# One bank more held back before a score tile is issued, in the last 24 visits of a fused attention and token-mixing kernel

## The chip, the cores and the metric

The kernel runs on one core of one Trainium2 chip. The metric is the device time of one launch in microseconds. Before the change three runs took 1613.73 to 1614.21 us, with a median of 1614.09 us.

## The reference, cut to what matters

```python
def _A_ref(x, wq, wk, wv, wo):            # 32 heads of 20, one key and one value for all of them
    q = (x @ wq).reshape(B, S, H, Dh).transpose(0, 2, 1, 3)
    k = x @ wk
    v = x @ wv
    scores = jnp.einsum("bhqd,bkd->bhqk", q, k) * (Dh ** -0.5)
    p = _softmax(scores, axis=-1)
    o = jnp.einsum("bhqk,bkd->bhqd", p, v)
    return o.transpose(0, 2, 1, 3).reshape(B, S, H * Dh) @ wo
def _B_ref(x, w1, b1, w2, b2):            # an MLP over the tokens
    h = _layernorm(x, axis=-1)
    u = _gelu(jnp.einsum("bsd,sf->bdf", h, w1) + b1)
    return (jnp.einsum("bdf,fs->bds", u, w2) + b2).transpose(0, 2, 1)
g = _sigmoid((x * gate_w).sum(-1, keepdims=True))
out = g * _A_ref(x, ...) + (1 - g) * _B_ref(x, ...)
```

S is 2048 tokens, D 640 channels, F 1728; everything is float32.

## The kernel before, in words

**Visits.** Attention is worked off in 32 units (4 blocks of 512 queries times 8 groups of 4 heads), and each unit in 16 visits, one for every 128 keys: 512 visits. A visit has four score tiles (line 643, a 62-row matmul of 128 keys by 512 queries), each followed by an exponential on ScalarE (line 652, `p<-...`), and then the product with v (line 754, written `PV` below) on the whole array. The softmax's row maxima are found ahead of time: line 494 makes score tiles with the queries as rows, and VectorE takes their maxima (line 500). The maxima of a whole unit go through lines 515 (VectorE), 517 to 519 (GpSimd), 526 (VectorE), 527 (a store to DRAM, on SyncE's queue) and 533 (the fetch back, on the same queue) into two rows of the unit's query tile, from which the score matmuls read them.

**Halves.** Score tiles and the long products of the MLP and of the output projection use only 64 of the array's 128 rows. Two of them run at the same time, one in the upper half (rows 0 to 63) and one in the lower (64 to 127). TensorE takes its instructions in one program order; an instruction that waits holds up everything behind it, of both halves.

**Banks.** PSUM has 8 banks of 128x512 float32, with the tile names `ms` (three), `s` (three), `g` and `o`. In the last stretch one of them (`o`) collects the products with v over all visits; the other seven go round between score tiles, tiles for row maxima, and the accumulators of the output projection. A bank comes free when the exponential, the maximum or the closing sum (line 934, VectorE) has read it.

**The last 24 visits.** The first 488 visits are arranged by the function `main`, the last 24 by a loop of their own from line 1230 on, in eight blocks of 2, 3, 3, 3, 3, 3, 3 and 4 visits. What stands beside the scores there is the output projection of the last tokens (`tail_job`, line 926): chains of half-array products (64x128 by 64x320), written `L926` below. Each chain opens an accumulator with its first product, and needs a free bank for it; the chain's end calls line 934. A block first issues its score tiles (`lanes[b]`, for half `b`; in the first two blocks the last tiles for row maxima too) and its share of the products (`fs[b]`, pairs of the instruction and of whether it opens an accumulator), mixed by the rule that is changed, and then the PV of its visits, back to back. The scores run one visit ahead of the PV. How many scores and products a block has in each half is settled before the mixing.

**The planner's clock.** `at[b]` is the planner's own time of half `b`; a score advances it by `X_US` 0.232 and a product by `F_US` 0.147. `pool` holds the free banks, each with the time at which the planner expects it to be free; `bank_take` takes the earliest, `bank_give` returns it with the time at which its reader should be done. `banks_at(t)` counts the banks that are free by `t`. The loop of one block:

```python
while any(lanes) or any(fs):
    b = 0 if at[0] <= at[1] and (lanes[0] or fs[0]) or not (lanes[1] or fs[1]) else 1
    soon = sum(any(first for _, first in f[:3]) for f in fs)
    score = lanes[b] and (not fs[b] or banks_at(at[b]) > soon)
    if score or fs[b][0][1]:
        at[b] = max(at[b], min(e for e, _ in pool))
    clock["now"] = at[b]
    if score:
        lanes[b].pop(0)()
        at[b] += X_US
    else:
        fs[b].pop(0)[0]()
        at[b] += F_US
```

So `soon` is the number of halves (0, 1 or 2) that open an accumulator among their next three products.

Of the kernel before, what the change touches and what calls it, by code (L numbers as in the profile page):

```python
# [44 lines left out]
def mix_kernel(ctx: ExitStack, tc: tile.TileContext, A_x, A_wq, A_wk, A_wv, A_wo,  # L45
# [436 lines left out]
    def ms_next(b):  # L482
        k = given[b]
        if k >= 32 * NU:
            return None
        given[b] += 1
        n, r = divmod(k, 32)
        (kq, pr), qt = divmod(r // 4, 2), r % 4

        def step():  # L490
            if n not in mtiles:
                mtiles[n] = mpool.tile([P, 16, 4], F32, name="mp")
            ms = lead_bank() if lead_banks else bank_take()
            nc.tensor.matmul(ms, qmax[n][64 * b:64 * b + 60, pr, qt * P:(qt + 1) * P],  # L494
                             kst[64 * b:64 * b + 60, kq * NB:(kq + 1) * NB], start=True, stop=True)
            if not lead_banks:
                bank_give(ms, "max")
            c = (2 * b + pr) * 4 + qt
            behind, last["ins"] = last["ins"], None
            r = nc.vector.tensor_reduce(mtiles[n][:, c, kq:kq + 1], ms, axis=AX.X, op=ALU.max)  # L500
            if behind is not None:
                tc.add_manual_dep(r.ins, behind.ins.name, SYNC, reason="row tiles that share a bank")
                last["sig"] = r
            issued[b] += 1
            if min(issued) == 32 * n + 1:
                new_qmax(n + 1)

        return step

    def ms_done():  # L510
        n = len(row_max)
        if n < NU and min(issued) >= 32 * (n + 1):
            mm = mmpool.tile([P, 16], F32, name="mm")
            busy("dve", 0.14)
            nc.vector.tensor_reduce(mm, mtiles.pop(n), axis=AX.X, op=ALU.max)
            mn = mmpool.tile([P, 2, 16], F32R, name="mn")
            nc.gpsimd.tensor_scalar(mm, mm, -1.0, None, op0=ALU.mult)
            nc.gpsimd.tensor_copy(mn[:, 0, :], mm)
            nc.gpsimd.tensor_sub(mn[:, 1, :], mm, f32(mn[:, 0, :]))
            row_max[n] = mn  # L520

    def store_max(n):
        mn = row_max[n]
        mt = mpool.tile([P, 32], F32, name="mt")
        busy("dve", 0.19)
        nc.vector.transpose(mt, f32(mn).rearrange("p j c -> p (j c)"))
        nc.sync.dma_start(out=m_scr[n].rearrange("m (i e) -> i m e", i=4), in_=mt)

    def fetch_max(n):
        src = m_scr[n].rearrange("(j b r) e -> b j (r e)", j=2, b=2)  # L530
        for b in range(2):
            rows = f32(qtiles[n][64 * b + 60:64 * b + 62])
            nc.sync.dma_start(out=rows.rearrange("j p q -> j (p q)"), in_=src[b])
# [90 lines left out]
    def s_next(b):  # L624
        j = sc[b]
        if j >= 2 * len(units):
            return None
        sc[b] += 1

        def step():  # L630
            qk(j // 2, j % 2, b)

        step.score = True
        return step
# [31 lines left out]
    at, skip, final = 0, 3, NS * PRO - 6  # L666
# [65 lines left out]
    def banks_at(t):  # L732
        return sum(e <= t for e, _ in pool)
# [151 lines left out]
    def tail_load(i, late=False):  # L885
        st, r0, r1 = jobs[i]
        cols = slice(st * P, (st + 1) * P)
        oT, yt = room(i)
        c1 = r1 // P
        for j in range(2):  # L890
            if r0:
                low = slice(r0 + j * MID // 2, r0 + (j + 1) * MID // 2)
                nc.sync.dma_start(out=f32(oT[:MID, j, 0]), in_=o_scr[j, r0:r1, cols])
                nc.sync.dma_start(out=f32(oT[MID:MID * 3 // 2, j, 0]), in_=o_scr[0, low, cols])
            elif not late:
                nc.sync.dma_start(out=f32(oT[:, j, :c1]), in_=o_scr[j, :c1 * P, cols].rearrange("(c p) s -> p c s", p=P))
            else:
                nc.sync.dma_start(out=f32(oT[:r1 - c1 * P, j, c1]), in_=o_scr[j, c1 * P:r1, cols])
        if r0 == 0 and not late:
            nc.sync.dma_start(out=yt, in_=y_scr[cols, :])  # L900
            if r1 < D:
                nc.gpsimd.memset(f32(oT[r1 - c1 * P:, :, c1, :]), 0.0)
        if late or r0 or r1 == D:
            loaded.append(i)

    def load_mid():
        for j, t in enumerate(wo_mid):
            for w, r0, r1, at in ((wo_hi, 0, MID, 0), (wo_lo, j * MID // 2, (j + 1) * MID // 2, MID)):
                while r0 < r1:
                    c, r = divmod(CUT + r0, P)  # L910
                    n = min(r1 - r0, P - r)
                    nc.sync.dma_start(out=f32(t[at:at + n]), in_=f32(w[r:r + n, c, :]))
                    r0, at = r0 + n, at + n
# [33 lines left out]
    def tail_take(h, n):  # L947
        out = []
        while len(out) < n and tail[h] and tail[h][0][0] in loaded:
            out.append(tail[h].pop(0)[1:])  # L950
        return out
# [54 lines left out]
    def full_last():  # L1006
        ws = [ev.tile([P, NB], F32, name="part", bufs=2) for _ in range(2)]
        for d, w in enumerate(ws):
            nc.gpsimd.memset(w[:, :HD2], 0.0)
            for hh in range(4):  # L1010
                r = (H - 4 + hh) * DH
                nc.sync.dma_start(out=w[32 * hh:32 * hh + DH, :HD2], in_=A_wo[r:r + DH, d * HD2:(d + 1) * HD2])
        return ws
# [79 lines left out]
    def settle(wide=False):  # L1093
        for _ in range(2 if spare[0] else 1):
            if later and (wide or spare[0] or not later[0][0]):
                f = later.pop(0)[1]
                if f:
                    f()
        pop_chain()
# [20 lines left out]
    lanes = [0.0, 0.0]  # L1120
# [109 lines left out]
    for j, n in enumerate(BLOCKS):  # L1230
        ends = [min(2 * len(units), 2 * (v + n) + 2) for _ in range(2)]
        lanes = [[], []]
        own = [(2 * len(units) - c + 32 * NU - m) * X_US for c, m in zip(sc, given)]
        while any(sc[b] < ends[b] for b in range(2)):
            b = int(sc[1] < sc[0])
            lanes[b].append(s_next(b))
        for b in range(2):
            more = -(-(32 * NU - given[b]) // max(1, LAST_M - j))
            for i in range(more):
                lanes[b].insert((i + 1) * len(lanes[b]) // (more + j), ms_next(b))  # L1240
        left = len(units) - v
        fs = [tail_take(b, len(tail[b]) if n == left else
                        max(0, round(((own[b] + len(tail[b]) * F_US) * n / left - len(lanes[b]) * X_US) / F_US)))
              for b in range(2)]
        at = [begin, begin]
        while any(lanes) or any(fs):
            b = 0 if at[0] <= at[1] and (lanes[0] or fs[0]) or not (lanes[1] or fs[1]) else 1
            soon = sum(any(first for _, first in f[:3]) for f in fs)
            score = lanes[b] and (not fs[b] or banks_at(at[b]) > soon)
            if score or fs[b][0][1]:  # L1250
                at[b] = max(at[b], min(e for e, _ in pool))
            clock["now"] = at[b]
# [6 lines that stand above are left out]
        begin = max(at) + 0.38 + n * 0.927  # L1259
        ms_done()  # L1260
        for _ in range(n):
            settle()
            pv_group([v], True)
            v += 1
        if NU - 1 in set(row_max) - sent:
            store_max(NU - 1)
            sent.add(NU - 1)
            fetch_max(NU - 1)
            back_in.add(NU - 1)
        if v - n < 492 <= v:  # L1270
            load_mid()
        if v - n < 498 <= v:
            w_full = full_last()
        if v >= 502 and len(loaded) < len(jobs):
            for i in range(len(loaded), len(jobs)):
                tail_load(i)
# [94 lines left out]
```

## Time and profile before

| what | before |
|---|---|
| median of 3 runs | 1614.09 us |
| time of the profiled execution | 1613.95 us |
| its span | 1612.2 us |
| TensorE busy | 1605.3 us (100%) |
| VectorE, ScalarE, GpSimd busy | 1355.9, 1308.0, 868.4 us |
| granted TensorE clock | 1.000 |
| stretch of the last 24 visits | 1531 to 1601 us of the span |

How to read it: the time is that of the whole launch, the span runs from the first to the last instruction in the trace, and 1.75 us lie around it. "Busy" of TensorE counts every moment at which at least one matmul is under way in either half, and the ends of matmuls are modelled; so a stretch in which one half stands still, or in which both do for a tenth of a microsecond, shows as busy.

### The profile page before, as it was taken

The page shows a single profiled execution, that of the slowest core. Times are in us where ns is not written, and L with a number is a line of the kernel's source. Part 1 is how long each engine was busy: PE and PEld are TensorE (multiplying, and loading weights), DVE is VectorE, ACT ScalarE, POOL GpSimd, SP SyncE. Part 2 cuts the span into 40 slices and gives each one's busy share as a digit, 9 for nine tenths or more (in the row PEclk, how much of TensorE's full clock was granted, in tenths as well). Part 3 has the DMA queues.
Part 4 walks back from the last instruction along what each step waited for, and adds up shares of the span by engine and source line. Part 5 has one row for each costly group of instructions (what it writes and reads, how often), then busy time and mean ns, then how long its engine had stood idle before and what let it go on. Part 6 is the DMA issues. An engine that isn't in the chain of part 4 may idle for free.

```text
span 1612.2 us, 39502 instructions
## 1 busy us (share of the span) xinstructions
PE 1605.3 (100%) x14865; PEld 1124.5 (70%) x14865; DVE 1355.9 (84%) x2344; ACT 1308.0 (81%) x2565; POOL 868.4 (54%) x977
## 2 busy tenths in 40 slices
PE   9999999999999999999999999999999999999998
PEld 7889777677767776666666666666666666666676
DVE  6689999999999999888888888888888888766643
ACT  4445888888888888888888888888888888999974
POOL 6568766778767777644544434454544433344420
PEclk9999999999999999999999999999999999999999
DMA  7655323223233323222222122222222212346421
GB/s 216 212 164 143 78 73 80 76 75 87 77 86 84 80 66 83 64 73 81 73 71 68 51 66 66 72 70 81 73 73 73 59 48 67 96 119 188 151 85 50
DMA packets 183750, 145.07 MB, mean 90 GB/s; under 512 B 38291, under 2 KB 145424, under 8 KB 183560
## 3 DMA queue, kind: packets, MB, share of 16 engines
q1 hardware_dynamic: 183272, 142.23, 31.6%
q8 instruction: 117, 1.92, 0.5%
q14 instruction: 73, 0.60, 0.1%
q10 hardware_dynamic: 288, 0.33, 0.1%
HBM read 108.75 MB, written 32.15 MB: 87 GB/s over the span
## 4 chain that ended last, share of the span: by engine, by line
PE 98%; DVE 1%; POOL 0%; ACT 0%; issue 0%; DVEq 0%; POOLq 0%
PE s L754 16%; PE g L832 11%; PE s L643 10%; PE ms L754 10%; PE g L1035 9%; PE ms L643 8%; PE ms L494 7%; PE s L494 6%; PE pp L303 4%; PE o L754 4%; PE o L643 3%; PE o L494 2%; PE s L686 2%; PE g L971 2%; PE ms L926 1%; DVE mp L500 1%
## 5 line engine op out<-in xcount | busy, mean ns | idle before, releaser
L500 DVE TENSOR_REDUCE mp<-ms 128x1 f32<-128x512 f32 x966 | 632.2, 680 | 59.3 <-PE ms L494 50.9
L652 ACT ACTIVATE p<-s 128x512 f32<-128x512 f32 x941 | 545.7, 618 | 44.5 <-PE ms L754 12.8
L500 DVE TENSOR_REDUCE mp<-s 128x1 f32<-128x512 f32 x756 | 499.8, 680 | 74.1 <-PE s L494 61.2
L652 ACT ACTIVATE p<-ms 128x512 f32<-128x512 f32 x817 | 482.2, 615 | 37.0 <-PE s L754 13.6
L767 POOL TENSOR_TENSOR acc<-acc,part 128x512 f32<-128x512 f32 x213 | 275.1, 1291 | 313.4 <-ACT part L766 300.7
L494 PE MATMUL ms<-kst,qmx 60*128 60x512 f32 x966 | 378.6, 413 | 0.1
L643 PE MATMUL s<-qst,kst 62*128 62x512 f32 x946 | 363.4, 408 | 0.2 <-DVE mp L500 0.2
L643 PE MATMUL ms<-qst,kst 62*128 62x512 f32 x822 | 322.2, 408 | 0.7 <-DMA qst<-m_scr 0.7
L1035 PE MATMUL g<-slot,wh 64*128 64x320 f32 x1344 | 306.1, 313 | 0.0
L494 PE MATMUL s<-kst,qmx 60*128 60x512 f32 x756 | 302.3, 413 | 0.0
L754 PE MATMUL s<-p,v_sb 128*32 128x512 f32 x2240 | 269.4, 598 | 0.0
L1035 PEld LDWEIGHTS g<-slot,wh 64*128 64x128 f32 x1344 | 216.7, 184 | 69.6 <-issue 52.0
L500 DVE TENSOR_REDUCE mp<-o 128x1 f32<-128x512 f32 x303 | 206.2, 681 | 42.9 <-PE o L494 41.4
L134 POOL TENSOR_TENSOR wl<-wr,wh 128x512 fp32r<-128x512 f32 (+1 forms) x176 | 218.0, 1239 | 30.6 <-ACT wh L131 15.4
L643 PEld LDWEIGHTS s<-qst,kst 62*128 62x128 f32 x946 | 174.1, 185 | 60.8 <-ACT p L652 27.0
L1035 PE MATMUL g<-slot,wl 64*128 64x320 f32 x672 | 205.4, 306 | 0.0
L832 PE MATMUL g<-u,wh 64*128 64x320 f32 x864 | 196.5, 309 | 0.0
L832 PE MATMUL g<-slot,wh 64*128 64x320 f32 x864 | 196.3, 309 | 0.0
L643 PEld LDWEIGHTS ms<-qst,kst 62*128 62x128 f32 x822 | 151.5, 186 | 46.8 <-ACT p L652 29.3
L494 PEld LDWEIGHTS ms<-kst,qmx 60*128 60x128 f32 x966 | 175.3, 185 | 4.2 <-DVE mp L500 0.4
L652 ACT ACTIVATE p<-o 128x512 f32<-128x512 f32 x264 | 162.7, 616 | 11.3 <-PE ms L754 7.1
L754 PE MATMUL ms<-p,v_sb 128*32 128x512 f32 x1344 | 161.6, 598 | 0.0
(250 smaller groups left out, 3078.6 us busy)
## 6 DMA issues: line engine op xcount, KB each, us to landing
wr<-in_B_w_dram SPq DMA_DIRECT2D x136, 256.0 KB
qmx<-q_scr SPq DMA_DIRECT2D x192, 80.0 KB
qst<-q_scr SPq DMA_DIRECT2D x192, 80.0 KB
ot<-l_scr SPq DMA_DIRECT2D x120, 64.0 KB
y_scr<-yo SPq DMA_DIRECT2D x16, 320.0 KB
slot<-o_scr SPq DMA_DIRECT2D x16, 320.0 KB
o_scr<-ot SPq DMA_DIRECT2D x124, 40.0 KB
o_scr<-acc SPq DMA_DIRECT2D x124, 40.0 KB
```

Source lines behind the costliest of these rows:

```text
L134: nc.gpsimd.tensor_sub(wl[:, :nv], wr[:, :nv], f32(wh[:, :nv]))
L303: nc.tensor.matmul(pp, w, t, start=first and n == 0, stop=not more and n == len(steps) - 1)
L494: nc.tensor.matmul(ms, qmax[n][64 * b:64 * b + 60, pr, qt * P:(qt + 1) * P], kst[64 * b:64 * b + 60, kq * NB:(kq + 1) * NB], start=True, s ...
L500: r = nc.vector.tensor_reduce(mtiles[n][:, c, kq:kq + 1], ms, axis=AX.X, op=ALU.max)
L643: nc.tensor.matmul(s, kst[64 * b:64 * b + 62, kb * P:(kb + 1) * P], q[64 * b:64 * b + 62, pr, :], start=True, stop=True)
L652: e = nc.scalar.activation(p, s, AF.Exp, scale=SCALE)
L686: nc.tensor.matmul(pu[r][:, :HD2], w[rows, c, :], h[rows, st, :], start=(st == 0 and k == 0), stop=(st == NS - 1 and k == 2))
L754: nc.tensor.matmul(o[32 * hh:32 * hh + 32, :], v_sb[:, kb + i, :], ptiles.pop((u, hh)), start=opened and i == 0, stop=(i == len(us) - 1) a ...
L767: nc.gpsimd.tensor_add(sums[0], sums[0], part)
L832: other_tile(half, nc.tensor.matmul(hold["p"][:, :HD2], w[r, i, :], u[d][r, fc, :], start=(hold["n"] == 1), stop=(hold["n"] == 6 * FC - 3)))
L971: other_tile(half, nc.tensor.matmul(hold["p"][:, :HD2], o[r, c, :], w[r, c, d * HD2:(d + 1) * HD2], start=(hold["n"] == 1), stop=(hold["n" ...
L1035: other_tile(half, nc.tensor.matmul(hold["p"][:, :HD2], w[r, st % HS, :], h[d][r, st, :], start=(hold["n"] == 1), stop=(hold["n"] == 6 * NS)))
```

## The change

A score tile (or a tile for row maxima, which goes through the same list) is issued only while more than `soon + 1` banks are free by the planner's clock, where more than `soon` were enough. A half that has no products left issues its scores as before.

```diff
             soon = sum(any(first for _, first in f[:3]) for f in fs)
-            score = lanes[b] and (not fs[b] or banks_at(at[b]) > soon)
+            score = lanes[b] and (not fs[b] or banks_at(at[b]) > soon + 1)
             if score or fs[b][0][1]:
                 at[b] = max(at[b], min(e for e, _ in pool))
```

The numbers of scores, maxima and products in each block and half stay what they were, as do the orders of GpSimd's and SyncE's instructions. On TensorE the mixture inside each of the eight blocks changes, and with it the banks that the tiles get. Two places follow.

On TensorE, the start of the fourth block, just behind the last product with v of the third. A row is one instruction (x2: two in a row): its line, its output tile, its inputs. `L643` is a score, `L926` a product; the half isn't shown. Before:

```order
L643 MATMUL ms<-qst,kst 128x512
L643 MATMUL s<-qst,kst 128x512
L643 MATMUL ms<-qst,kst 128x512
L643 MATMUL s<-qst,kst 128x512
L643 MATMUL ms<-qst,kst 128x512
L926 MATMUL g<-slot_84,u_1163 128x320 x2
L926 MATMUL s<-slot_84,u_1163 128x320
L926 MATMUL g<-slot_84,u_1163 128x320
L926 MATMUL s<-slot_84,u_1163 128x320
L926 MATMUL g<-slot_84,u_1163 128x320
L926 MATMUL s<-slot_84,u_1163 128x320
L926 MATMUL g<-slot_84,u_1163 128x320
```

The same place after:

```order
L643 MATMUL ms<-qst,kst 128x512
L643 MATMUL g<-qst,kst 128x512
L643 MATMUL s<-qst,kst 128x512 x2
L926 MATMUL ms<-slot_84,u_1163 128x320
L926 MATMUL s<-slot_84,u_1163 128x320
L926 MATMUL ms<-slot_84,u_1163 128x320
L926 MATMUL s<-slot_84,u_1163 128x320
L926 MATMUL ms<-slot_84,u_1163 128x320
L926 MATMUL s<-slot_84,u_1163 128x320
L926 MATMUL ms<-slot_84,u_1163 128x320
L926 MATMUL s<-slot_84,u_1163 128x320
```

Before, five scores stand ahead of the first product, and with the two accumulators (`g` and `s`) that makes seven banks; after, four scores stand there, and the fifth comes behind five products of its half. The blocks 3 and 5 to 8 start in the same two ways.

On VectorE, around the end of the second block: `L500` are the last row maxima of the last unit, `L934` the closing sums of accumulators (a pair for each half of an output tile), `L515` and `L526` the steps that follow the last maximum. Before:

```order
L934 SCALAR_TENSOR_TENSOR yo<-g,g_col,yo 128x320
L500 TENSOR_REDUCE mp<-ms 128x1 x3
L934 SCALAR_TENSOR_TENSOR yo<-s,g_col,u_1163 128x320
L934 SCALAR_TENSOR_TENSOR yo<-s,g_col,yo 128x320
L500 TENSOR_REDUCE mp<-s 128x1
L515 TENSOR_REDUCE mm<-mp 128x16
L526 STREAM_TRANSPOSE mt<-mn 128x32
```

After:

```order
L934 SCALAR_TENSOR_TENSOR yo<-g,g_col,yo 128x320
L500 TENSOR_REDUCE mp<-s 128x1
L500 TENSOR_REDUCE mp<-g 128x1
L500 TENSOR_REDUCE mp<-ms 128x1
L934 SCALAR_TENSOR_TENSOR yo<-ms,g_col,u_1163 128x320
L934 SCALAR_TENSOR_TENSOR yo<-ms,g_col,yo 128x320
L500 TENSOR_REDUCE mp<-s 128x1
L500 TENSOR_REDUCE mp<-g 128x1
L515 TENSOR_REDUCE mm<-mp 128x16
L526 STREAM_TRANSPOSE mt<-mn 128x32
```

One more maximum stands behind the second pair of sums than before, so two maxima instead of one follow it ahead of `L515`.

## The prediction

> **What bounds the kernel now.** I read the page's chain first, then the busy time in the eight blocks of the last 24 visits, then one block instruction by instruction. The chain that ended last, by engine:
>
> ```profile
> PE 98%; DVE 1%; POOL 0%; ACT 0%; issue 0%; DVEq 0%; POOLq 0%
> ```
>
> TensorE's instruction stream is the kernel; a tenth of a microsecond taken out of it comes off the time. The change reaches only the stretches of the last 24 visits in which scores and products are mixed. They are, as the chain in order of time has them, the stretches between the end of one run of PV and the start of the next (columns: length; busy time and count of TensorE, its weight loads, VectorE, ScalarE, GpSimd; TensorE's granted clock; DMA share; GB/s):
>
> ```profile
> 1531.41:1535.45 4.04, 4.04 (x47) 3.69 (x50) 3.15 (x5) 3.99 (x9) 3.77 (x4) 1.00 0.19 76
> 1537.31:1543.53 6.22, 6.22 (x69) 5.70 (x73) 4.98 (x9) 5.76 (x12) 0.02 (x1) 1.00 0.30 78
> 1546.24:1552.24 6.00, 6.00 (x72) 5.52 (x75) 2.05 (x4) 5.47 (x12) 0.00 (x0) 1.00 0.30 70
> 1554.95:1560.93 5.98, 5.98 (x72) 5.52 (x75) 2.40 (x5) 5.51 (x12) 0.00 (x0) 1.00 0.02 4
> 1563.65:1569.60 5.95, 5.95 (x71) 5.54 (x75) 1.46 (x4) 5.49 (x12) 2.51 (x4) 1.00 0.30 69
> 1572.31:1578.34 6.03, 6.03 (x72) 5.61 (x76) 1.73 (x4) 5.57 (x12) 0.00 (x0) 1.00 0.27 75
> 1581.05:1586.95 5.90, 5.90 (x71) 5.43 (x74) 2.20 (x4) 5.43 (x12) 0.00 (x0) 1.00 0.01 3
> 1589.66:1597.83 8.17, 8.17 (x97) 7.41 (x100) 3.55 (x7) 5.99 (x12) 0.00 (x0) 1.00 0.01 2
> ```
>
> The eight lengths add up to 48.3 us. All of them read as 100% busy, which hides the question: whether both halves of the array work all the time. The timeline of TensorE in the fourth block tells (start, duration, line, output<-inputs):
>
> ```profile
> 1554.88 0.50 PE L643 MATMUL ms<-qst,kst 62*128 62x512 f32 x1
> 1554.88 0.50 PE L643 MATMUL s<-qst,kst 62*128 62x512 f32 x1
> 1555.22 0.40 PE L643 MATMUL ms<-qst,kst 62*128 62x512 f32 x1
> 1555.22 0.40 PE L643 MATMUL s<-qst,kst 62*128 62x512 f32 x1
> 1555.45 0.39 PE L643 MATMUL ms<-qst,kst 62*128 62x512 f32 x1
> 1555.46 0.45 PE L926 MATMUL g<-slot,u 64*128 64x320 f32 x2
> 1555.68 0.31 PE L926 MATMUL s<-slot,u 64*128 64x320 f32 x1
> ...
> 1555.98 0.31 PE L926 MATMUL s<-slot,u 64*128 64x320 f32 x1
> ...
> 1556.13 0.43 PE L643 MATMUL ms<-qst,kst 62*128 62x512 f32 x1
> ...
> 1557.54 0.50 PE L643 MATMUL s<-qst,kst 62*128 62x512 f32 x1
> ...
> 1557.88 0.41 PE L643 MATMUL g<-qst,kst 62*128 62x512 f32 x1
> ...
> 1558.44 0.50 PE L643 MATMUL s<-qst,kst 62*128 62x512 f32 x1
> ...
> 1559.45 0.30 PE L926 MATMUL s<-slot,u 64*128 64x320 f32 x1
> ...
> 1560.04 0.31 PE L926 MATMUL s<-slot,u 64*128 64x320 f32 x1
> ...
> 1560.48 0.45 PE L926 MATMUL ms<-slot,u 64*128 64x320 f32 x2
> 1560.86 0.64 PE L754 MATMUL o<-p,v_sb 128*32 128x512 f32 x4
> ```
>
> Four numbers come out of it. A product takes its half 0.1475 us (1559.45 to 1560.04 are four steps). A score takes 0.233 (1555.22 to 1555.45 to 1555.68 in the first half, 0.46 for two). The block's first score takes 0.34, 0.107 more, and lasts 0.50 instead of 0.39 or 0.40. From the last product (the second of 1560.48, so 1560.63) to the first PV it is 0.23, 0.08 more than a product's step.
>
> With these the least length of a block is known, since the program's order tells how many scores and products each half gets: in the fourth block 6 and 27 in one, 6 and 28 in the other. The fuller half needs 6 x 0.233 + 28 x 0.1475 = 5.53, and with 0.107 and 0.08 it is 5.72. It took 5.98; 0.26 are waits. The same for each block (scores and products of the fuller half: 7 and 14; 10 and 22; 6 and 28 in blocks 3 to 6; 6 and 27; 6 and 40) gives least lengths of 3.88, 5.76, four times 5.72, 5.57 and 7.49, together 45.6. **The eight blocks hold 2.7 us that are neither work nor unavoidable**: 0.16, 0.46, 0.28, 0.26, 0.23, 0.31, 0.33 and 0.68. That is all that another mixture can gain.
>
> **What makes up the 2.7 us.** The readers of the banks in the fourth block, ScalarE's exponentials and VectorE's first sums:
>
> ```profile
> 1555.42 0.60 ACT L652 ACTIVATE p<-ms 128x512 f32<-128x512 f32 x1 [2.66 <-PE s L643]
> 1555.91 0.59 ACT L652 ACTIVATE p<-s 128x512 f32<-128x512 f32 x1
> 1556.39 0.60 ACT L652 ACTIVATE p<-ms 128x512 f32<-128x512 f32 x1
> 1556.86 0.62 ACT L652 ACTIVATE qmx<-s 128x512 f32<-128x512 f32 x1
> ...
> 1557.18 0.55 DVE L934 SCALAR_TENSOR_TENSOR yo<-g,g_col,u 128x320 f32<-128x320 f32 x1 [1.47 <-PE g L926]
> 1557.83 0.55 DVE L934 SCALAR_TENSOR_TENSOR yo<-s,g_col,yo 128x320 f32<-128x320 f32 x1
> ```
>
> The exponentials begin 0.54 after the first score and follow every 0.48; a bank is back 0.60 later. Five scores and two accumulators take all seven banks by 1555.68. The sixth score, due at 1556.13 (0.15 behind the product of 1555.98), needs the first exponential's bank, which ends at 1556.02, and lasts 0.43 instead of 0.39. The score of 1557.54 needs the fourth exponential's (1556.86 + 0.62 = 1557.48); the one of 1558.44 needs the second sum's (1557.83 + 0.55 = 1558.38). Each starts 0.06 behind its bank's last reader, lasts 0.50 like a block's first score, and holds up the next score of its half: 1557.54 to 1557.88 are 0.34 where 0.233 would do. So even a wait of a few hundredths costs about 0.1 us, and the instructions of the other half behind it come late as well.
>
> **The change part by part.** It removes and adds no instruction. It moves the fifth score of a block behind five products or more (the fourth block's order shows it), and so leaves a bank free at each later issue.
>
> Walked through for the fourth block, in time from its first score: scores at 0 and 0.34 in both halves, then products from 0.575. The exponentials still begin at 0.54 and free banks at 1.20, 1.68, 2.17 and 2.66 (0.06 behind the ends above). Two accumulators and four scores leave one bank free, and the fifth score, at 0.575 + 5 x 0.1475 = 1.31, finds that one and the bank of 1.20. The next two accumulators open at about 2.0 and 2.1 and find the other one and that of 1.68. The next scores come at about 2.7 and 2.9 and find the banks of 2.17 and 2.66; the ones after that, from 3.2 on, the sums' banks, from about 2.9. Nothing waits: the block takes its least 5.72, and 0.26 are gained.
>
> The same walk, with the same durations (0.43 from a score's start to an idle reader's, which is the 0.54 without the first score's 0.107; 0.65 from sum to sum; 0.69 a maximum, from a row further down), through the other new blocks leaves ten waiting instructions: four in block 2, one each in 3 and 5, two each in 6 and 8. They cost 0.22, 0.11, 0.07, 0.27 and 0.15, together 0.8. Some blocks now end with a lone score in one half, where before they ended with products in both; I put 0.2 for that over all blocks. **The sum: 2.7 gone, 0.8 + 0.2 back, 1.7 us gained.** This is an estimate, and its ends are 2.7 (nothing waits any more) and 0 (as many waits as before, at other places); below 0 one mechanism is known, which is the slower rival. I take the walk's value, since the fourth block's waits come out of the same steps as the trace has them.
>
> What is moved later is covered. A score that comes later makes its exponential later, but the last four scores of a block belong to the next block's PV, and ScalarE's twelve exponentials at 0.48 take 5.8 of the 8.7 us between the starts of the fourth and the fifth block. In the last block, whose scores are all needed, the last scores now stand ahead of some 16 products of their half, 2.3 us, and the fourth visit's PV is last in its run. SyncE's and GpSimd's orders don't move. VectorE's sums move with the products; their readers wait for nothing near.
>
> One rule of the Trainium skill bears on the mixture. Two products of one half that follow each other directly are the pair of 1555.46: 0.45 for both, so 0.31 for one and 0.15 to the next, no more than across the halves. The Trainium skill (TensorE: Matmul & The Clock Gate, Part 3, The mechanism) says that a weight load overlaps with running matmuls only when its row group differs, so each such pair would show a load; the trace disagrees. By that rule, with 62 direct neighbours of one half in the old order and 53 in the new, 9 x 0.107 = 1.0 us more would be gained; I leave it out of the sum.
>
> **The rivals.** (1) *The waits only move* (no gain, 1613.6 to 1614.4 us). The planner's clock runs from its own estimate of each block's start, and where it is off by a tenth the spare bank is counted wrongly. For it: in the old order the clock let the sixth score go at the very moment its bank came back. Against: one whole bank more is about 0.48 us of slack, one exponential's step, and the waits are hundredths.
>
> (2) *All waits go* (2.7 us, 1611.4). For it: the fourth block's walk. Against: the second block, where five tiles for maxima go round beside the twelve scores, and the last.
>
> (3) *The last unit's maxima come late* (slower). The last maximum goes through VectorE, GpSimd, a store and a fetch; until that has landed, TensorE's whole queue stands at the first score of the last unit, in the third block. The chain, on VectorE, SyncE's queue and TensorE:
>
> ```profile
> 1542.47 0.69 DVE L500 TENSOR_REDUCE mp<-s 128x1 f32<-128x512 f32 x1
> 1543.20 0.22 DVE L515 TENSOR_REDUCE mm<-mp 128x16 f32<-128x64 f32 x1
> 1544.37 0.21 DVE L526 STREAM_TRANSPOSE mt<-mn 128x32 f32<-128x32 f32 x1 [0.95 <-POOL mn L519]
> 1544.61 0.56 SPq L527 DMA_DIRECT2D m_scr<-mt  x1
> 1546.58 0.53 SPq L533 DMA_DIRECT2D qst<-m_scr  x2
> 1548.65 0.42 PE L643 MATMUL s<-qst,kst 62*128 62x512 f32 x1
> 1548.91 0.47 PE L643 MATMUL g<-qst,kst 62*128 62x512 f32 x1
> ```
>
> The score of 1548.91 is the first reader, 5.75 us behind the end of the last maximum (1543.16), and it came 0.26 behind the score before it in its half, so it waited at most 0.03. In the new order the third block starts about 0.4 earlier and the reader stands 3.4 us into it, at 1549.2, so there are at least 0.3 us of room; the last maximum, now with another one ahead of it behind the second pair of sums, is due between the same time and 0.6 later. At 0.6 this costs 0.3. Slower than before it gets from a delay of 2.0 on; two more pairs of sums ahead of the maxima (four times 0.65) would be 2.6, and the kernel 0.6 slower, 1614.7. To be 0.2% slower takes 5.3 us of delay, about a whole second chain.
>
> **How the numbers follow.** The profiled execution took 1613.95 us, 0.14 less than the median of 1614.09. It would take 1613.95 - 1.7 = 1612.25, and the median 1612.4 us. Chances: the forecast, 0.9 to 2.4 us gained, 0.64; rival 1 0.16; rival 2 0.08; rival 3 0.08; 0.04 for something that the trace doesn't show. The range takes in rivals 1 and 2 and the near part of 3: 1611.3 to 1614.5. A difference of 0.2% is 3.2 us, about what a measurement of this kernel can tell from no change. The forecast and rivals 1 and 2 lie within it, since the blocks hold only 2.7; beyond it on the faster side I leave 0.06, for something outside the blocks, and on the slower side 0.07, mostly rival 3 at its worst.
>
> **What would show it.** Right: the eight stretches add up to about 46.6 us instead of 48.3, the fourth is near 5.72, and scores of 0.43 to 0.50 behind a block's first pair become rare. Right in mechanism but wrong in size: they are rare, yet the blocks keep their lengths. Wrong: a gap before a score in the third block that ends with the fetch of the maxima, PV that waits for an exponential, or a difference outside 1531 to 1601 us.

## The result, and the profile after

The changed kernel takes 1611.7 us (median of 22 runs, 1610.99 to 1612.22), the kernel before, timed beside it, 1613.72 (22 runs, 1613.46 to 1614.21): a ratio of 0.9987, with a 95% interval of 0.9981 to 0.9993, which leaves out 1. That is 2.0 us less: faster, by less than the 0.2% that the prediction names. The profiled execution took 1611.67 us with a span of 1609.9.

The eight stretches of the last 24 visits after the change, from the first score's start to the first PV's start (length; busy time and count of TensorE, its weight loads, VectorE, ScalarE, GpSimd; granted clock; DMA share; GB/s), and their sum:

```profile
1531.13:1535.05 3.92, 3.92 (x46) 3.59 (x43) 2.73 (x5) 3.75 (x8) 2.24 (x3) 1.00 0.11 37
1536.90:1542.81 5.91, 5.91 (x69) 5.46 (x65) 4.47 (x8) 5.03 (x10) 1.10 (x1) 1.00 0.32 81
1545.53:1551.44 5.91, 5.91 (x72) 5.39 (x68) 2.03 (x4) 5.20 (x11) 0.00 (x0) 1.00 0.33 83
1554.15:1559.85 5.70, 5.70 (x72) 5.34 (x68) 2.34 (x4) 5.17 (x11) 0.00 (x0) 1.00 0.02 6
1562.56:1568.27 5.71, 5.71 (x71) 5.42 (x67) 1.46 (x4) 5.12 (x11) 2.53 (x4) 1.00 0.28 66
1570.99:1576.92 5.93, 5.93 (x73) 5.32 (x69) 2.00 (x4) 5.16 (x11) 0.00 (x0) 1.00 0.34 104
1579.63:1585.19 5.56, 5.56 (x71) 5.28 (x67) 2.20 (x4) 4.94 (x10) 0.00 (x0) 1.00 0.01 3
1587.90:1595.56 7.66, 7.66 (x97) 7.31 (x94) 3.30 (x6) 6.03 (x12) 0.00 (x0) 1.00 0.01 2
sum 46.30, PE 46.30 PEld 43.11 DVE 20.54 ACT 40.41 POOL 5.87; mean PE 5.79 PEld 5.39 DVE 2.57 ACT 5.05 POOL 0.73
```

48.3 us have become 46.3: 2.0 us, as much as the median moved. Every block is shorter. Blocks 4, 5 and 7 stand at their least lengths (5.72, 5.72, 5.57), block 8 went from 8.17 to 7.66. The two spans differ by 2.3, but 0.2 of that is the start of the first block, 1531.34 before and 1531.13 after, in a part that the change doesn't touch; over the ten profiled executions told of below that start lies anywhere from 1531.05 to 1532.16. So the stretches, whose sum differs by 0.03 us at most between two profiles of one kernel (below), are the better measure of so small a change than one execution's time.

The fourth block after, on TensorE, beside the rows of before in the prediction:

```profile
1554.15 0.49 PE L643 MATMUL ms<-qst,kst 62*128 62x512 f32 x1
1554.15 0.50 PE L643 MATMUL g<-qst,kst 62*128 62x512 f32 x1
1554.48 0.39 PE L643 MATMUL s<-qst,kst 62*128 62x512 f32 x2
1554.71 0.31 PE L926 MATMUL ms<-slot,u 64*128 64x320 f32 x1
...
1555.45 0.39 PE L643 MATMUL ms<-qst,kst 62*128 62x512 f32 x1
...
1556.77 0.39 PE L643 MATMUL s<-qst,kst 62*128 62x512 f32 x1
...
1557.00 0.39 PE L643 MATMUL s<-qst,kst 62*128 62x512 f32 x1
...
1557.30 0.39 PE L643 MATMUL ms<-qst,kst 62*128 62x512 f32 x1
...
1559.85 0.64 PE L754 MATMUL o<-p,v_sb 128*32 128x512 f32 x4
```

The fifth score comes 1.30 us into the block and lasts 0.39; before, the sixth, 1.25 us in, lasted 0.43, and two later ones 0.50. Behind the first pair no score of this block is long any more. The same holds for the eight stretches together: of the 86 tiles for scores and maxima behind the blocks' first pairs, 28 lasted 0.43 us or more before and 5 after; of the 432 products, of which most last 0.30 or 0.31, 20 lasted 0.34 or more before and 5 after.

### The profile page after: what moved, and what is told of

The parts are those of the page before. It is cut to its first block, busy times and chain, and to the rows that moved or that the text cites. A ratio compares the mean times of both kernels' runs of the same rounds, so it can differ in the third digit from the quotient of the medians.

```text
span 1609.9 us, 39500 instructions
## 1 busy us (share of the span) xinstructions
PE 1603.3 (100%) x14865; PEld 1121.9 (70%) x14865; DVE 1356.4 (84%) x2344; ACT 1309.3 (81%) x2565; POOL 869.6 (54%) x977
## 4 chain that ended last, share of the span: by engine, by line
PE 98%; DVE 1%; POOL 0%; issue 0%; ACT 0%; DVEq 0%; POOLq 0%
PE s L754 16%; PE g L832 12%; PE s L643 10%; PE ms L754 10%; PE g L1035 9%; PE ms L643 8%; PE ms L494 7%; PE s L494 5%; PE pp L303 4%; PE o L754 4%; PE o L643 3%; PE o L494 2%; PE s L686 2%; PE g L971 2%; DVE mp L500 1%; PE s L926 1%
## 5 line engine op out<-in xcount | busy, mean ns | idle before, releaser
L500 DVE TENSOR_REDUCE mp<-ms 128x1 f32<-128x512 f32 x965 | 631.7, 680 | 57.6 <-PE ms L494 43.2
L500 DVE TENSOR_REDUCE mp<-s 128x1 f32<-128x512 f32 x755 | 499.4, 681 | 74.5 <-PE s L494 52.7
L643 PE MATMUL s<-qst,kst 62*128 62x512 f32 x944 | 362.7, 408 | 0.2 <-DVE mp L500 0.2
L643 PE MATMUL ms<-qst,kst 62*128 62x512 f32 x826 | 323.9, 406 | 0.1
L500 DVE TENSOR_REDUCE mp<-o 128x1 f32<-128x512 f32 x303 | 206.3, 681 | 42.8 <-PE o L494 36.9
L643 PEld LDWEIGHTS s<-qst,kst 62*128 62x128 f32 x944 | 173.3, 185 | 60.7 <-ACT p L652 27.1
L643 PEld LDWEIGHTS ms<-qst,kst 62*128 62x128 f32 x826 | 152.6, 185 | 43.8 <-ACT p L652 29.4
```

Source lines behind the costliest of these rows:

```text
L643: nc.tensor.matmul(s, kst[64 * b:64 * b + 62, kb * P:(kb + 1) * P], q[64 * b:64 * b + 62, pr, :], start=True, stop=True)
```

## The experiments

My theory is that the time went in waits at banks, each with about 0.1 us of a weight load that a waiting instruction can't hide. Two scores of the fourth block of the kernel before show what that means, by the rows of their weight loads (`PEld`) and of the matmuls themselves (`PE`):

```profile
1557.54 0.18 PEld L643 LDWEIGHTS s<-qst,kst 62*128 62x128 f32 x1
1557.54 0.50 PE L643 MATMUL s<-qst,kst 62*128 62x512 f32 x1
...
1557.59 0.50 PE L926 MATMUL ms<-slot,u 64*128 64x320 f32 x2
...
1558.08 0.18 PEld L643 LDWEIGHTS ms<-qst,kst 62*128 62x128 f32 x1
1558.23 0.40 PE L643 MATMUL ms<-qst,kst 62*128 62x512 f32 x1
```

The first waited for its bank: its load and its matmul start together, and the matmul lasts 0.50. The pair of products behind it in the other half takes 0.50, where other pairs take 0.45. The second score, at 1558.23, didn't wait: its load started 0.15 earlier, beside running products, and the matmul lasts 0.40.

The rivals: (A) holding back more is simply better; (B) the gain comes from the changed neighbours in the two halves, by the rule on weight loads that the prediction weighed; (C) a whole bank is needed, not the hundredths by which a bank came late; (D) all of it is the fifth score at a block's start. Direct neighbours are two instructions of one half that follow each other directly, counted in a kernel's order of issue within the eight stretches. The edits are made to the kernel before, unless told otherwise, and each of the first seven kernels told of was timed once. The lengths of the eight stretches, read from each kernel's TensorE timeline, in us:

| kernel | 1 | 2 | 3 | 4 | 5 | 6 | 7 | 8 | sum |
|---|---|---|---|---|---|---|---|---|---|
| before | 4.04 | 6.23 | 6.00 | 5.98 | 5.95 | 6.03 | 5.90 | 8.17 | 48.3 |
| after | 3.92 | 5.91 | 5.91 | 5.70 | 5.71 | 5.93 | 5.56 | 7.66 | 46.3 |
| two held back | 4.53 | 6.98 | 5.95 | 5.73 | 6.13 | 5.72 | 5.74 | 7.48 | 48.3 |
| one fewer held back | 5.47 | 7.87 | 10.07 | 10.19 | 8.66 | 10.19 | 10.04 | 10.59 | 73.1 |
| banks counted 0.1 late | 3.91 | 5.78 | 5.86 | 5.95 | 5.92 | 6.09 | 5.63 | 8.16 | 47.3 |
| first scores only | 4.04 | 5.98 | 5.90 | 5.91 | 5.96 | 6.02 | 5.94 | 8.14 | 47.9 |
| later scores only | 3.92 | 6.12 | 5.80 | 5.71 | 5.71 | 5.94 | 5.67 | 7.90 | 46.8 |
| six banks, old rule | 4.28 | 6.74 | 6.02 | 6.17 | 6.13 | 6.15 | 6.01 | 8.85 | 50.4 |
| after, maxima later | 3.92 | 5.92 | 6.71 | 5.71 | 5.71 | 5.93 | 5.56 | 7.66 | 47.1 |
| rule by block | 3.90 | 5.77 | 5.78 | 5.71 | 5.71 | 5.71 | 5.58 | 7.47 | 45.6 |

**Two banks more held back.**

```diff
-            score = lanes[b] and (not fs[b] or banks_at(at[b]) > soon)
+            score = lanes[b] and (not fs[b] or banks_at(at[b]) > soon + 2)
```

> Two banks more are held back instead of one (more than soon + 2). Waits at banks (my theory): the scores pile up at the ends of blocks 1, 2, 5 and 7, where they must wait for each other's banks, while blocks 4, 6 and 8 lose their last waits; the eight stretches add up to 48.7 us (before 48.3, after 46.3), blocks 1 and 2 to 11.3 instead of 9.8 after, block 8 to 7.5. Rival A (whatever holds more banks back is better): 46.0 or less. Rival B (the gain comes from fewer direct neighbours of one half, 0.107 us each; before 62, after 53, here 43): about 45.3.

Measured: 48.3 in the stretches and 1614.05 us (before beside it 1614.17). The pattern by block is the one expected, 11.5 us in blocks 1 and 2, 7.48 in block 8. The first two stretches:

```profile
1531.53:1536.06 4.53, 4.28 (x46) 3.51 (x43) 2.92 (x5) 3.64 (x8) 3.92 (x5) 1.00 0.20 77
1537.91:1544.89 6.98, 6.89 (x69) 5.62 (x65) 5.05 (x9) 4.71 (x10) 0.14 (x1) 1.00 0.41 122
```

TensorE now even stands idle for 0.25 and 0.09 us (the length less the busy time): the products run out and the scores that were held back wait for each other's banks. Rivals A and B fall: with the most held back and the fewest direct neighbours of one half (43), the gain is gone.

**One bank fewer held back.**

```diff
-            score = lanes[b] and (not fs[b] or banks_at(at[b]) > soon)
+            score = lanes[b] and (not fs[b] or banks_at(at[b]) > soon - 1)
```

> One bank fewer is held back than before (more than soon - 1), so with no opening near a score goes whenever its turn comes. Waits at banks: scores go one behind the other at the start of each block, at the pace of the exponentials and the maxima, with TensorE standing in between; the eight stretches add up to about 68 us, 20 more than before, and each of blocks 3 to 7 to 8.5 or more. Rival B (direct neighbours: 53 here, as after): 46 to 47.

Measured: 73.1, and 1639.53 us. The sign and the place are as expected, against rival B, which has as many neighbours here as after (53). The size is 5 us above my number. Block 5, at 8.66, is near what I expected; blocks 3, 4, 6 and 7 took 1.4 to 1.5 us more, and there the granted clock fell (last section).

**The old rule, with banks counted 0.1 us late.**

```diff
-            score = lanes[b] and (not fs[b] or banks_at(at[b]) > soon)
+            score = lanes[b] and (not fs[b] or banks_at(at[b] - 0.1) > soon)
```

> The old rule (more than soon), but a bank counts as free only 0.1 us after the planner's time for it. Waits at banks: the old waits were a few hundredths each, paid with 0.1 more for the weight load, so 0.1 us of caution already removes about half of them: the stretches add up to 47.2 us (before 48.3, after 46.3); blocks 1, 3 and 7 reach 3.9, 5.8 and 5.6, blocks 5, 6 and 8 keep their length. Rival C (a whole spare bank is needed): 48.3. Rival B (66 direct neighbours): 48.7.

Measured: 47.3, with blocks 1, 3 and 7 at 3.91, 5.86 and 5.63, and 5, 6 and 8 unchanged or within 0.06. Half of the gain needs no spare bank, only 0.1 us of caution; so half of the old waits were shorter than that, and cost what they cost through what a wait brings with it. Rival C falls for this half. The caution is asked of scores alone: 7 of the 28 long scores and maxima are left, but 15 of the 20 long products. In block 8, which gains nothing, the waits are those of products that open accumulators: in the kernel before they start at 1590.84 and 1591.33, each 0.05 behind the end of an exponential, and last 0.41. Whether the other half needs a whole bank isn't shown, since no more than 0.1 us was tried. Rival B falls too: with 66 direct neighbours, 4 more than before, the stretches are 1.0 shorter. The single time, 1613.56, is only 0.6 below the kernel before, with the first block at 1531.93, 0.6 later than in the profile of before.

**The new rule for a block's first scores only,** and **for its later scores only.** The first applies `+ 1` until the block's first product is out, the second from the third product on (`done` counts the products; the second's other lines are those of the first):

```diff
-        at = [begin, begin]
+        at, done = [begin, begin], 0
...
-            score = lanes[b] and (not fs[b] or banks_at(at[b]) > soon)
+            score = lanes[b] and (not fs[b] or banks_at(at[b]) > soon + (not done))
...
             clock["now"] = at[b]
+            done += not score
```

> The new rule only until a block's first product is issued, the old one from there on: the fifth score is moved behind the first products, the rest is mixed as before. Waits at banks: waits in the middle of the blocks stay, 47.8 us in all, block 8 unchanged at 8.2. Rival D (the gain is the fifth score that no longer takes the last bank at the block's start): 46.3, as after. Rival B (78 direct neighbours): 50.

```diff
-            score = lanes[b] and (not fs[b] or banks_at(at[b]) > soon)
+            score = lanes[b] and (not fs[b] or banks_at(at[b]) > soon + (done > 1))
```

> The old rule until two products of a block are issued, the new one from there on: the five scores at the start stay, the later scores are held back. Waits at banks: most of the gain without the block's start, 47.2 us in all (before 48.3, after 46.3), of it block 2 at 6.4 and block 8 at 8.0, the others within 0.1 of their least lengths. Rival D (it is the fifth score at the start): 48.3. Rival B (direct neighbours of one half; 85 here, 62 before): 50.7.

Measured: 47.9 and 46.8 (1613.59 and 1612.11 us). The sums of the two, as the windows give them:

```profile
sum 47.89, PE 47.89 PEld 44.37 DVE 21.34 ACT 42.25 POOL 6.12; mean PE 5.99 PEld 5.55 DVE 2.67 ACT 5.28 POOL 0.76
```

```profile
sum 46.77, PE 46.77 PEld 43.12 DVE 20.54 ACT 40.60 POOL 5.84; mean PE 5.85 PEld 5.39 DVE 2.57 ACT 5.08 POOL 0.73
```

The start alone brings 0.4, the later scores alone 1.5, together 1.9 of the 2.0; the two parts add up, and three quarters lie in the middle of the blocks. Rival D falls, though the fifth score was the first thing that I saw in the order. For the later scores my number was 0.4 too high, nearly all of it in block 2 (6.12 instead of 6.4) and block 8 (7.90 instead of 8.0); block 6, at 5.94, is 0.2 above its least length, where I expected 0.1 at most.

The numbers for rival B in these two expectations and in the next are wrong. Within the stretches the three kernels have 47, 54 and 60 direct neighbours, 31 fewer than the 78, 85 and 91 given, while the counts of 62, 53, 43 and 66 hold. (32 matmuls behind the last visits follow one another in one stream, which makes 31 pairs; probably those were counted in.) From 48.3 at 62 neighbours, and by its price of 0.107 us each, rival B then asks for 46.7, 47.4 and 48.1 us. It is off by 1.2, 0.7 and 2.3, and it has the order of the first two the wrong way round.

**One bank taken away, with the old rule.**

```diff
     otile.append(bank_take())
+    unused = bank_take()
...
+    pool.append((1e9, unused))
     o = otile[0]
     banks = [t for _, t in sorted(pool, key=lambda x: x[0])] + [o]
```

> The old rule with one of the seven banks taken out of the round until the last block is done; the program's work is the same. Waits at banks: the stretches add up to 50.6 us, 2.3 more than before, the most in block 8 (about 8.8). If banks were not what is short: 48.3. Rival B (91 direct neighbours): 51.4, spread evenly.

Measured: 50.4 and 1615.71 us, block 8 at 8.85, the most of all blocks. Banks are what is short: nothing else was changed but the mixture that follows from it, and a bank less costs as much as a bank's caution brings. Rival B, by the right count, asks for a little less than before (60 direct neighbours against 62), and its even spread isn't there either (block 3 lost 0.02, block 8 0.68).

**The new kernel with the last unit's maxima made later.** The last step on VectorE behind the maxima is done seven times:

```diff
-            nc.vector.tensor_reduce(mm, mtiles.pop(n), axis=AX.X, op=ALU.max)
+            src = mtiles.pop(n)
+            for _ in range(7 if n == NU - 1 else 1):
+                nc.vector.tensor_reduce(mm, src, axis=AX.X, op=ALU.max)
```

> The new kernel, with the last step on VectorE behind the last maximum (0.22 us) done seven times instead of once for the last unit, so that the fetch of the maxima comes some 1.3 us later. It measures the room of the third rival of the prediction: with the 0.3 us of room that I gave it, the third block is about 1.0 us longer than after (5.9), 6.9, and the rest unchanged. With more room than 1.3 the third block stays at 5.9.

Measured: the third block 6.71, 0.80 longer, the rest the same. The fetch on SyncE's queue and its first reader on TensorE, after and in this kernel (its line numbers are 2 higher):

```profile
1546.57 0.53 SPq L533 DMA_DIRECT2D qst<-m_scr  x2
...
1548.92 0.39 PE L643 MATMUL ms<-qst,kst 62*128 62x512 f32 x1
```

```profile
1548.38 0.53 SPq L535 DMA_DIRECT2D qst<-m_scr  x2
...
1550.12 0.47 PE L645 MATMUL ms<-qst,kst 62*128 62x512 f32 x1 [0.53 <-ACT p L654]
```

From the third block's start (1545.53 and 1545.83) the fetch goes out 1.04 and 2.55 in, 1.51 later; the reader starts 3.39 and 4.29 in, 0.90 later. So 0.6 us of the delay did no harm: that is the room, if beyond it TensorE waits one for one, which a single delay can't show. The row puts the idle time down to ScalarE, but what moved here is the fetch. The rival's mechanism is real, its room was twice what I gave it, and it is far from what it would take.

**A rule by block.** For each block the caution that left the fewest waits when the new order was walked through with the trace's durations:

```diff
-            score = lanes[b] and (not fs[b] or banks_at(at[b]) > soon)
+            score = lanes[b] and (not fs[b] or banks_at(at[b] - (0, 0.1, 0.1, 0, 0, 0, 0, 0)[j]) > soon + (1, 0, 1, 1, 1, 2, 1, 2)[j])
```

> For each block the caution that leaves the fewest waits in the walk with the trace's durations: one bank more, except block 2 (the old rule with banks counted 0.1 us late), block 3 (one more, counted 0.1 late), and blocks 6 and 8 (two more). Waits at banks: 45.9 us in the eight stretches against 46.3 after and 45.6 at least, so 0.4 us below the new kernel and 2.4 below the old, about 1611.3 us. If what is left after is not waits at banks: 46.3 and 1611.7.

Measured: 45.6 in the stretches, 0.3 less than I expected, and 1611.22 us (11 runs), a ratio of 0.9982 (0.9973 to 0.9991) to the kernel before. Once more, beside the new kernel on one chip:

> The new kernel beside the next one on one chip. Waits at banks: eight stretches of 46.3 us and about 2.0 us below the kernel before.

> The rule by block once more, beside the new kernel. Waits at banks: 45.6 us in the stretches, 0.6 below the new kernel and 2.7 below the kernel before. If the difference between the two was one between chips or sessions, the same time as the new kernel.

```profile
sum 46.29, PE 46.29 PEld 43.09 DVE 20.55 ACT 40.40 POOL 5.84; mean PE 5.79 PEld 5.39 DVE 2.57 ACT 5.05 POOL 0.73
```

```profile
sum 45.66, PE 45.66 PEld 43.01 DVE 21.02 ACT 39.51 POOL 5.83; mean PE 5.71 PEld 5.38 DVE 2.63 ACT 4.94 POOL 0.73
```

The stretches repeat: 46.29 and 45.66. The times are 1612.27 (1611.69 to 1612.6; ratio 0.9988, 0.9979 to 0.9997) and 1611.39 (1611.16 to 1611.91; ratio 0.9983, 0.9974 to 0.9992); 0.9 us apart, though the two intervals against the kernel before overlap. With 45.6 the blocks are at the sum of their least lengths. Behind the first pairs two scores still last longer than 0.43 us and no product longer than 0.32; so next to nothing is left of the waits, and nothing else was in the 2.7 us. This order has 57 direct neighbours, 4 more than that of the new kernel, and is 0.6 shorter: once more not what rival B asks for.

## Why the prediction was right

**The bound.** That the blocks hold 2.7 us which are neither work nor unavoidable was the base of the sum. The rule by block reaches 45.6, the least length that the prediction gave, so 2.7 was the whole of it.

**The mechanism.** Shown by three kinds of experiment that each change one thing in the rule or the banks: a bank less costs 2.1 us, 0.1 us of caution brings 1.0, and half the rule brings its part. The walk through the fourth block came out within 0.02 us for the fifth score (1.31, measured 1.30) and the length (5.72, measured 5.70), and within 0.08 for the next scores (2.7 and 2.9, measured 2.62 and 2.85).

**The give-back.** The term that was mis-sized: 0.8 for waits and 0.2 for uneven ends, 1.0 in all; measured 0.7, which is 46.3 less 45.6. The waits I expected in blocks 2, 5 and 6 cost 0.15, nothing and 0.21 instead of 0.22, 0.07 and 0.27; those in blocks 3 and 8 cost a little more, 0.19 and 0.17 instead of 0.11 and 0.15. Block 3 has one waiting score more than the walk found. Both stand in the half that ends last, starting at 1547.71 and 1548.34:

```profile
1547.71 0.47 PE L643 MATMUL s<-qst,kst 62*128 62x512 f32 x1
...
1548.34 0.49 PE L643 MATMUL s<-qst,kst 62*128 62x512 f32 x1
```

The walk left ten waiting instructions, and ten matmuls were long, not all in the same blocks. So the waits took 0.7 of the 0.8, and of the 0.2 for uneven ends next to nothing shows. Hence 2.0 instead of 1.7, and 1611.7 instead of 1612.4; the rest of that difference is the kernel before, whose median was 0.37 lower over these 22 runs than over the three shown first, whose times are among the 22. (A slip that changes nothing: by the prediction's own terms a delay of the maxima of 5.2 us, not 5.3, would make the kernel 0.2% slower.)

**The rivals.** The waits did not just move: what is left of them is a quarter, in time, and a fifth in long matmuls (10 instead of 48). The late maxima had 0.6 us of room instead of 0.3, and the new kernel's fetch goes out at the same time as before (1546.57 and 1546.58). Of the Trainium skill's rule (TensorE: Matmul & The Clock Gate, Part 3, The mechanism) that a weight load hides only behind matmuls of another row group nothing shows in the stretches: they got 1.0 us shorter with 4 direct neighbours more (66, banks counted late), 0.6 shorter than after with 4 more (57, rule by block), and no shorter than before with 19 fewer (43, two held back).

## What to carry to other kernels

Where several users draw on a few buffers through a schedule that is planned by a clock, leave it one buffer or a tenth of a microsecond of slack: a wait of hundredths cost about 0.1 us here, through the weight load that it uncovered, and an instruction that waits holds up the other half too. More slack isn't better, since what is held back piles up at the end of the stretch. An engine that reads as 100% busy can still hold such time; compare a stretch with the sum of its fuller half's steps, and judge a change of a thousandth by the stretches rather than by single times.

## What the runs showed that I had not expected

In the kernel with one bank fewer held back the granted clock halved while TensorE kept working. The third block in five pieces (the granted clock is the third number from the end):

```profile
1550.08:1553.50 3.42, 3.14 (x14) 1.39 (x10) 0.00 (x0) 2.83 (x6) 0.00 (x0) 1.00 0.25 63
1553.50:1554.00 0.50, 0.50 (x2) 0.22 (x1) 0.00 (x0) 0.50 (x2) 0.00 (x0) 0.87 0.64 174
1554.00:1557.00 3.00, 3.00 (x21) 2.74 (x22) 0.55 (x1) 2.66 (x6) 0.00 (x0) 0.50 0.43 110
1557.00:1557.50 0.50, 0.50 (x9) 0.50 (x8) 0.00 (x0) 0.00 (x0) 0.00 (x0) 0.72 0.07 10
1557.50:1560.15 2.65, 2.65 (x36) 2.46 (x33) 1.46 (x3) 0.00 (x0) 0.00 (x0) 1.00 0.01 4
```

At first one score starts every 0.49 us, at the exponentials' pace:

```profile
1551.32 0.49 PE L643 MATMUL s<-qst,kst 62*128 62x512 f32 x1 [0.28 <-ACT p L652]
1551.81 0.49 PE L643 MATMUL g<-qst,kst 62*128 62x512 f32 x1
1552.30 0.50 PE L643 MATMUL s<-qst,kst 62*128 62x512 f32 x1
1552.79 0.50 PE L643 MATMUL ms<-qst,kst 62*128 62x512 f32 x1
...
1556.03 0.47 PE L926 MATMUL s<-slot,u 64*128 64x320 f32 x1
...
1557.48 0.31 PE L926 MATMUL s<-slot,u 64*128 64x320 f32 x1
```

Then the clock is 0.50 from about 1553.87 (0.87 is 0.37 us of 1.00 and 0.13 of 0.50) to 1557.28, 3.41 us, and the products in it last 0.47 instead of 0.31. There was no idle stretch of that length: the row with 0.28 us of waiting for ScalarE has the longest gap before a score here. The mean over the block is 0.83, as in blocks 4, 6 and 7; blocks 5 and 8 crawl as well, with no such fall. What decides between them no run here shows.
